# Filter copies between GpSimd's DMA issues in batch 0 of a fused Fourier filter and GELU MLP

## The chip, the cores and the metric

The kernel runs on one core of a Trainium2 chip. The metric is the device time of one execution in microseconds (us). TensorE is called PE, VectorE DVE, ScalarE ACT, GpSimd POOL, SyncE SP, as in the profile.

## The reference

`x` has 8 batches of 3008 rows and 256 columns. Each column is filtered in the frequency domain along the rows, and the result goes through an MLP with an exact GELU:

```
X = rfft(x, axis=1)
Y = X * (filt_r + 1j * filt_i)
y = irfft(Y, n=3008, axis=1)             # then reshaped to (24064, 256)
h = y @ w_in                              # (256, 2048)
g = 0.5 * h * (1 + erf(h / sqrt(2)))
out = g @ w_out                           # (2048, 256)
```

Inputs and output are float32. The filters have 1505 frequencies and 256 columns each.

## The kernel before

The transform of 3008 = 47 x 64 rows is done as matrix products in four stages, with tables of sines that the kernel computes at its start. The product with the filters lies in the middle. The MLP is done in tiles of 512 rows: `mm1` (line 711) makes a tile of `h`, ACT applies GELU into `g_sb` (line 714), and `mm2` (lines 727 and 793) multiplies by `w_out_sb`.

All order is written out by hand: each engine runs its instructions in the order in which the program names them, and instructions of different engines wait for each other by semaphores. Batch 0 goes first and alone. From batch 1 on, the stages of the next batch are put into numbered slots between the `mm1` and `mm2` of the present one; sixteen slots make a tile, and `mm2` of tile 0 begins in slot 10. The first stage of batch 1 (line 498) stands in slots 4, 8, 11 and 13, and its folds on DVE (lines 158 and 159) in slots 0, 1, 5 and 8.

The change is in batch 0. Its steps, with the lines of the profile:

- `load_x` (line 95): POOL issues eight DMAs that load batch 0 of `x` and cast it to bf16.
- `warm_up(n)` (line 375): `n` spare matmuls of 128 x 512 on PE, whose results nobody reads.
- `table_2_sin` (328), `table_2_swap` (335 on PE, copied by ACT), `table_3` (352, eight transposes on PE into one PSUM bank), `table_3_copy` (381 on ACT, into the tile `T3`), `table_3_turn` (368, two DVE instructions that make `T3i` out of `T3` with the parts swapped and signs turned), `table_4` (343): the tables. The trace shortens the names of these tiles to `T`.
- `c1` (606): the first stage, sixteen calls `u`, of four matmuls each, which are copied to `y_sb` in turn by DVE (383) and ACT (381).
- `load_filters(k0, k)` (168): POOL issues four DMAs for frequency groups `k0` to `k0 + k`: the real plane twice (32 partitions straight, 32 mirrored), then the imaginary plane twice. They fill partitions 0 to 63 of the tile `F`.
- `load_w_in` (211): two DMAs of 512 KB, one for each half of `w_in_sb`.
- `dup_filters(engine, k0, k)` (186): copies partitions 0 to 63 of `F` to 64 to 127, two groups at a time.
- `move_filters` (179): SP's DMAs that copy filters into the order `Fu` of the later batches.
- `c1t(q, ...)` (621): transposes of `y_sb` on PE, sixteen for `c1t(0)` and `c1t(1)` together, copied to `b_sb` by DVE or ACT.
- `c2(p)` (636, then 640 or 645 on DVE): two matmuls and the product with groups `2p` and `2p + 1` of `F`, for `p` from 0 to 11. Product `p` needs the filter copy of its two groups.
- `c3`, `c3t`, `c4` (658, 673, 687): the way back. Then come `mm1` and the slots.
- `load_x_pairs` (104): after its copies, POOL issues twelve DMAs with batch 1 of `x`, and then `load_w_out` (216), two DMAs of 512 KB, the first with the rows that `mm2` reads first.

POOL does its DMA issues and its copies in program order, and its DMAs go through one queue (software_dynamic). An issue also waits until an earlier DMA on the same semaphore has landed; there are eight such semaphores, taken in turn.

Before the change POOL issues all twelve filter DMAs and both of `w_in`, clears a corner of `vt_sb`, and then copies groups 6 to 23. Groups 0 to 3 are copied by DVE, groups 4 and 5 by ACT, after the last `c1`. DVE runs `table_3_turn(0)` after `c1` call 11.

Of the kernel before, what the change touches and what calls it, by code (L numbers as in the profile page):

```python
# [27 lines left out]
def _dram(src, off, dims):  # L28
    return dataclasses.replace(src, offset=src.offset + off, ap=[list(d) for d in dims])


class _Mix:
# [125 lines left out]
        tt(out=s[0:n], in0=x[0:n, 0, k], in1=x[0:n, 1, k], op=ALU.add)  # L158
        tt(out=x[0:n, 1, k], in0=x[0:n, 0, k], in1=x[0:n, 1, k], op=ALU.subtract)

    def load_filters(self, k0, k):

        nc, D = self.nc, self.D
        for t, src in enumerate((self.filt_r, self.filt_i)):
            direct = _dram(src, k0 * D, [[NA * D, 32], [D, k], [1, D]])
            mirror = _dram(src, (NA - k0) * D, [[NA * D, 32], [-D, k], [1, D]])
            for q, a in enumerate((direct, mirror)):
                nc.gpsimd.dma_start(out=self.F[32 * q:32 * q + 32, t, k0:k0 + k, :], in_=a)
# [36 lines left out]
                                     in_=_dram(self.x, 0, [[n, 2], [1, HB * self.D]]))  # L205
        self.load_x_mirror(b + 1, c, h)

    def load_w_in(self):
        wi = self.w_in.rearrange("(dc p) j -> p dc j", p=128)
        for dc in range(2):  # L210
            self.nc.gpsimd.dma_start(out=self.w_in_sb[:, dc, :], in_=wi[:, dc, :])

    def load_w_out(self, j):

# [647 lines left out]
def kernel(  # L862
# [9 lines left out]
    m = _Mix(ctx, tc, x, filt_r, filt_i, moe_w_in, moe_w_out, out)  # L872
    nc, B, S = tc.nc, m.B, m.S
# [6 lines left out]
    act = "act"  # L880
# [24 lines left out]
    t3 = m.pg.tile([128, 2, K1, 2, NB], BF16, tag="g", name="T3")  # L905
    m.T3, m.T3i = t3[:, 0], t3[:, 1]
    m.vt = m.pg.tile([128, 2, 97, 32], BF16, tag="g", name="vt_sb")
    for k, n in ((0, 6), (6, 8), (14, 10)):
        m.load_filters(k, n)
    m.load_w_in()  # L910

    nc.gpsimd.memset(m.vt[:, :, 96, :], 0.0)


    m.table_2_sin(0)
    for u in range(16):
        m.c1(u // 2, u % 2, False if u in (1, 3, 5, 7, 8, 10, 12, 14) else act)
        if u == 3:
            m.warm_up(3)
            m.table_2_swap(0)  # L920
            m.table_2_angle(g, 1)
            m.T1q = g.tile([2 * NA, K1, 2, 2], BF16, name="T1q")
            nc.vector.tensor_copy(out=m.T1q, in_=m.T1.rearrange("p (h r k) -> p k r h", h=2, r=2))
        if u == 7:
            m.table_2_sin(1)
            m.table_3(0)
            m.table_3_copy(0, 0)
            m.warm_up(2)
        if u == 11:
            m.table_2_swap(1)  # L930
            m.table_4(m.T4c, m.T1q, m.wtc, "n", False)
            m.table_3_turn(0)
            m.warm_up(1)
    m.table_3(1)
    m.dup_filters(nc.vector, 0, 2)
    m.dup_filters(nc.scalar, 4, 2)
    m.warm_up(1)
    m.c1t(0, (False, act))
    m.dup_filters(nc.vector, 2, 2)
    m.dup_filters(nc.gpsimd, 6, 18)  # L940
    m.move_filters(0, 2)
    m.c1t(1, (act,))
    m.table_3_copy(1, 0)
# [139 lines left out]
    for s in range((NT + 1) * 16):  # L1083
        t, jc = s // 16, s % 16
# [3 lines left out]
        if t - 1 in seven:  # L1088
            n = lambda i: (14 * i if i < 3 else 42 + 70 * (i - 3) // 13) if t == late else 7 * i
            m.mm2_seven(t - 1, n(jc), n(jc + 1))  # L1090
        elif t < 2:
            n = lambda i: max(4 * i - 40, 0) if i < 16 else min(24 + 8 * (i - 16) // 3, 64)
# [36 lines left out]
```

## Time and profile before

| | |
|---|---|
| time, median of 3 runs | 729.67 us (729.65 to 729.81) |
| profiled execution | 730.79 us |
| its span, first to last instruction | 728.7 us |
| PE busy | 712.0 us, 98% of the span |
| DVE, ACT, POOL busy | 84%, 79%, 35% |
| mean granted PE clock | 0.998 |
| chain that ended last | PE 93%, ACT 3%, others 1% or less |

The profile is of one execution, which took 1.12 us longer than the median of the timed ones. A row of a timeline has the start, the duration, the engine, the line, the operation, its tiles and shapes, and in square brackets how long the engine had been idle before it and what it then waited for. Ends of matmuls are modelled and overlap, so starts tell more than durations. Durations of POOL are rough.

### The profile page before, as it was taken

To read this page: it belongs to the slowest core of one execution; us is meant where nothing else is said; L and a number is where in the kernel's file an instruction comes from. 1 tells how busy PE (TensorE), PEld (TensorE's weight loads), DVE (VectorE), ACT (ScalarE), POOL (GpSimd) and SP (SyncE) were. 2 spreads that over 40 slices of the span, in tenths; PEclk is the share of its full clock that TensorE was granted. 3 is DMA by queue.
4 is the path that set the end of the run, shared out by engine and by line. 5 is a ranking of instruction groups with operands and counts; after the bars stand their busy time and mean duration, and the time that the engine had idled before them with its cause. 6 is when DMAs were issued, how large, how long until landed. Compare 5 with 4: busy or idle time off the path is not lost.

```text
span 728.7 us, 22436 instructions
## 1 busy us (share of the span) xinstructions
PE 712.0 (98%) x9189; PEld 507.4 (70%) x9341; DVE 613.4 (84%) x1105; ACT 576.6 (79%) x1050; POOL 256.9 (35%) x495
## 2 busy tenths in 40 slices
PE   8999999999999999999999999999999999999998
PEld 5856676666777666666777667666777767777776
DVE  7987788899998989898997999979988897765666
ACT  6998678788887888778887788877888788777773
POOL 7845847443232332223412242125521221121110
PEclk9999999999999999999999999999999999999999
DMA  9886634955257543665537654356545443311011
GB/s 154 157 179 145 160 95 118 238 135 116 82 166 193 124 110 97 187 151 134 127 104 190 144 132 122 88 153 158 104 101 140 139 123 100 94 47 43 31 58 59
DMA packets 88297, 91.05 MB, mean 125 GB/s; under 512 B 13169, under 2 KB 71537, under 8 KB 88193
## 3 DMA queue, kind: packets, MB, share of 16 engines
q1 hardware_dynamic: 63267, 51.21, 25.9%
q0 software_dynamic: 24512, 38.21, 23.4%
q8 instruction: 73, 1.20, 0.7%
q14 instruction: 29, 0.24, 0.1%
q10 hardware_dynamic: 416, 0.20, 0.1%
HBM read 57.48 MB, written 49.81 MB: 147 GB/s over the span
## 4 chain that ended last, share of the span: by engine, by line
PE 93%; ACT 3%; issue 1%; DVE 1%; DMA 1%; POOL 1%; DVEq 0%; POOLq 0%
PE ps_o L793 41%; PE ps_h L711 39%; PE ps_s L585 3%; PE ps_o L727 2%; ACT g_sb L714 2%; PE ps_s L556 2%; PE ps_s L525 2%; ACT y_sb L381 1%; DMA x_sb<-in_x_dram 1%; PE ps_s L498 1%; PE ps_s L142 1%; PE ps_c L658 1%; PE ps_warm L375 0%; PE ps_c L636 0%; PE ps_c1t L621 0%
## 5 line engine op out<-in xcount | busy, mean ns | idle before, releaser
L714 ACT ACTIVATE g_sb<-ps_h 128x512 f16<-128x512 f32 x752 | 446.1, 602 | 135.8 <-PE ps_h L711 111.4
L711 PE MATMUL ps_h<-y_sb,w_in_sb 128*128 128x512 bf16 (+3 forms) x1452 | 414.4, 365 | 0.7 <-ACT g_sb L714 0.3
L840 POOL DMA_DIRECT2D out_dram<-ost x219 | 124.2, 574 | 366.3 <-DVE ost L822 362.3
L793 PEld LDWEIGHTS <-g_sb 128*128 128x128 f16 x2880 | 188.8, 98 | 80.5 <-issue 12.4
L711 PEld LDWEIGHTS <-w_in_sb 128*128 128x128 bf16 x1600 | 125.6, 98 | 7.4 <-issue 1.6
L793 PE MATMUL ps_o<-w_sums,g_sb 128*128 128x128 f16 x1440 | 124.5, 219 | 1.6 <-DVE g_sb L765 0.2
L793 PE MATMUL ps_o<-w_sums,s_sb 128*128 128x128 f16 x1440 | 124.0, 219 | 1.8
L793 PEld LDWEIGHTS <-s_sb 128*128 128x128 f16 x1440 | 97.2, 98 | 38.0 <-issue 2.1
L759 DVE TENSOR_TENSOR s_sb<-g_sb 128x1024 f16<-128x1024 f16 x180 | 117.4, 683 | 1.0 <-ACT g_sb L714 0.6
L793 PE MATMUL ps_o<-w_out_sb,g_sb 128*128 128x128 f16 x1440 | 116.3, 219 | 1.9
L536 DVE TENSOR_TENSOR p<-ps_s,Fu 128x1024 bf16<-128x1024 f32 x84 | 101.7, 1217 | 13.7 <-PE ps_s L525 11.2
L765 DVE TENSOR_TENSOR g_sb<-s_sb,g_sb 128x1024 f16<-128x1024 f16 x90 | 61.7, 687 | 1.5
L793 PE MATMUL ps_o<-w_out_sb,F 128*128 128x128 f16 x704 | 60.6, 219 | 1.0
L775 DVE TENSOR_TENSOR F<-g_sb 128x1024 f16<-128x1024 f16 x88 | 60.0, 682 | 0.0
L793 PEld LDWEIGHTS <-F 128*128 128x128 f16 x704 | 47.1, 98 | 14.6 <-issue 0.4
L585 PEld LDWEIGHTS <-d_sb 96*128 96x128 bf16 x448 | 31.4, 97 | 26.7 <-issue 1.3
L822 DVE TENSOR_TENSOR ost<-t_sb,ps_o 128x256 f32<-128x256 f32 x88 | 32.9, 415 | 18.2 <-PE ps_o L793 18.2
L815 DVE TENSOR_TENSOR t_sb<-t_sb,ps_o 128x256 f32<-128x256 f32 x45 | 18.7, 416 | 32.2 <-PE ps_o L793 31.5
L381 ACT ACTIVATE y_sb<-ps_s 128x376 bf16<-128x376 f32 x95 | 45.4, 478 | 0.1
L381 ACT ACTIVATE F<-ps_s 128x512 bf16<-128x512 f32 x81 | 44.5, 608 | 0.1
L585 PE MATMUL ps_s<-F,d_sb 96*128 96x94 bf16 x448 | 37.2, 204 | 0.9
L810 DVE TENSOR_TENSOR ost<-t_sb,ps_o 128x256 f32<-128x256 f32 x45 | 18.6, 414 | 22.8 <-PE ps_o L793 22.8
(176 smaller groups left out, 630.3 us busy)
## 6 DMA issues: line engine op xcount, KB each, us to landing
out_dram<-ost POOLq DMA_DIRECT2D x117, 128.0 KB, 3.1
b_sb<-R SPq DMA_DIRECT2D x21, 512.0 KB
R<-F SPq DMA_DIRECT2D x84, 128.0 KB
R<-a_sb SPq DMA_DIRECT2D x108, 96.0 KB
d_sb<-R SPq DMA_DIRECT2D x54, 192.0 KB
x_sb<-in_x_dram POOLq DMA_DIRECT2D x36, 96.0 KB, 3.5
x_sb<-xr SPq DMA_DIRECT2D x32, 96.0 KB
x_sb<-in_x_dram POOLq DMA_DIRECT2D x12, 188.0 KB, 4.8
```

The costliest lines, as they stand in the source:

```text
L381: self.nc.scalar.activation(out=out, in_=in_, func=AF.Copy, scale=1.0 if scale is None else scale)
L536: v(out=w[:, a], in0=ps.unsqueeze(2).to_broadcast([128, 2, 2, 256]), in1=f.unsqueeze(1).to_broadcast([128, 2, 2, 256]), op=ALU.mult)
L585: nc.tensor.matmul(ps[:, 94 * i:94 * i + 94], lhsT=d[:, (grp % 2) * 4 + i, 128 * half:128 * half + 128], rhs=self.T4a[:, 4 * grp + i, 0:2 ...
L711: nc.tensor.matmul(ps[:, o:o + n], lhsT=w[:, dc], rhs=self.ring[:, dc, off:off + n], start=(dc == 0), stop=(dc == 1))
L714: nc.scalar.activation(out=self.st["g", t][:, jc, :], in_=ps, func=AF.Gelu)
L759: self.nc.vector.tensor_tensor(out=self.st["s", t][:, i:i + 2], in0=a, in1=b, op=ALU.subtract)
L765: self.nc.vector.tensor_tensor(out=a21[:, k], in0=self.st["s", t][:, k, 0], in1=a22[:, k], op=ALU.add)
L775: self.nc.vector.tensor_tensor(out=self.st["s4"][:, k], in0=a12[:, k], in1=s2[:, k], op=ALU.subtract)
L793: nc.tensor.matmul(ps[:, (m + 1) % 2, sub, :], lhsT=a[:, i, 128 * sub:128 * sub + 128], rhs=b[:, i], start=i == 0, stop=i == 7)
L815: v(out=t3, in0=t1, in1=p0, op=ALU.subtract)
L822: v(out=c(h, 1 - h), in0=tt, in1=p, op=ALU.add)
L840: eng.dma_start(out=out, in_=tile_[lo - r0:lo - r0 + n])
```

## The change

POOL issues the imaginary plane of the last filter groups only after it has copied groups 2 to 5, and `w_in` in two parts: the first half behind the copies of groups 6 to 15, the second behind those of groups 16 to 23. The clearing of `vt_sb` goes ahead of the filters. DVE keeps only the copy of groups 0 and 1, and makes it behind `c1t(0)`; ACT makes none. `table_3_turn(0)` goes behind the last `c1`. Two spare matmuls are added after the first swap and two before the wait for the second half of `x`, and one is removed ahead of `c1t(0)`.

```diff
-    def load_filters(self, k0, k):
+    def load_filters(self, k0, k, planes=(0, 1)):
...
-        for t, src in enumerate((self.filt_r, self.filt_i)):
+        for t in planes:
+            src = self.filt_i if t else self.filt_r
...
-    def load_w_in(self):
+    def load_w_in(self, dc):
         wi = self.w_in.rearrange("(dc p) j -> p dc j", p=128)
-        for dc in range(2):
-            self.nc.gpsimd.dma_start(out=self.w_in_sb[:, dc, :], in_=wi[:, dc, :])
+        self.nc.gpsimd.dma_start(out=self.w_in_sb[:, dc, :], in_=wi[:, dc, :])
...
-    for k, n in ((0, 6), (6, 8), (14, 10)):
-        m.load_filters(k, n)
-    m.load_w_in()
-
     nc.gpsimd.memset(m.vt[:, :, 96, :], 0.0)
-
+    m.load_filters(0, 6)
+    m.load_filters(6, 8)
+    m.load_filters(14, 10, (0,))
+    m.dup_filters(nc.gpsimd, 2, 4)
+    m.load_filters(14, 10, (1,))
+    m.dup_filters(nc.gpsimd, 6, 10)
+    m.load_w_in(0)
+    m.dup_filters(nc.gpsimd, 16, 8)
+    m.load_w_in(1)
...
             m.table_2_swap(0)
+            m.warm_up(2)
             m.table_2_angle(g, 1)
...
             m.table_3_copy(0, 0)
-            m.warm_up(2)
+            m.warm_up(4)
         if u == 11:
             m.table_2_swap(1)
             m.table_4(m.T4c, m.T1q, m.wtc, "n", False)
-            m.table_3_turn(0)
             m.warm_up(1)
+    m.table_3_turn(0)
     m.table_3(1)
+    m.c1t(0, (False, act))
     m.dup_filters(nc.vector, 0, 2)
-    m.dup_filters(nc.scalar, 4, 2)
-    m.warm_up(1)
-    m.c1t(0, (False, act))
-    m.dup_filters(nc.vector, 2, 2)
-    m.dup_filters(nc.gpsimd, 6, 18)
     m.move_filters(0, 2)
```

## The prediction, made before the change was run

> **What bounds the kernel now.** I read the page first: PE is busy 98% of the span and the chain that ended last is 93% PE. So a stage has room only where PE stands still or runs slowly, and whatever moves PE at the end of batch 0 moves the end by as much. Then I read the clock by stretches, the chain from 11 us, DVE and ACT up to the first product, POOL's queue, and the landing of `w_out`.
>
> The windows, in two stretches (busy time of each engine, granted clock, DMA share, GB/s):
>
> ```profile
> core 0: us, PE busy (x) PEld busy (x) DVE busy (x) ACT busy (x) POOL busy (x), PEclk, DMA share, GB/s
> 9.98:13.39 3.41, 2.15 (x26) 1.36 (x26) 1.77 (x5) 3.20 (x6) 1.45 (x4) 1.00 1.13 195
> 13.39:16.81 3.42, 3.42 (x33) 3.14 (x33) 2.36 (x7) 2.23 (x5) 3.42 (x7) 0.50 1.18 191
> ```
>
> After a stretch in which PE had 2.15 us of work, it runs 3.42 us at half clock. The chain there:
>
> ```profile
> 11.00 0.14 issue
> ...
> 13.35 1.11 PE ps_c L606 x12
> 14.46 0.85 PE ps_t L352 x8
> 15.32 0.43 PE ps_warm L375
> 15.74 1.46 PE ps_c1t L621 x16
> 17.20 0.23 PE ps_c L636 x2
> ```
>
> PE itself is the chain up to the first product. DVE and ACT wait there (idle before, in brackets):
>
> ```profile
> 13.21 0.34 DVE L368 TENSOR_SCALAR T<-T,turn_r 128x512 bf16<-128x512 bf16 x1
> 13.47 0.36 DVE L368 TENSOR_SCALAR T<-T,turn_i 128x512 bf16<-128x512 bf16 x1
> 13.76 1.00 DVE L383 CAST y_sb<-ps_c 128x384 bf16<-128x384 f32 x2
> 16.21 0.42 DVE L383 COPY b_sb<-ps_c1t 128x512 bf16<-128x512 bf16 x1 [0.83 <-PE ps_c1t L621]
> 17.46 1.23 DVE L640 TENSOR_TENSOR p<-ps_c,F 128x1024 bf16<-128x1024 f32 x1 [0.38 <-PE ps_c L636]
> ```
>
> From 17.46 DVE runs twelve products back to back, 1.13 us apart. POOL's queue decides what is loaded when:
>
> ```profile
> 14.81 1.26 POOL L168 DMA_DIRECT2D F<-in_filt_i_dram  x2
> 16.07 1.14 POOL L211 DMA_DIRECT2D w_in_sb<-in_moe_w_in_dram  x2
> 18.11 3.98 POOL L186 COPY F<-F 64x1024 bf16<-64x1024 bf16 x4 [0.74 <-DMA F<-in_filt_i_dram]
> 22.39 4.97 POOL L186 COPY F<-F 64x1024 bf16<-64x1024 bf16 x5 [0.31 <-DMA F<-in_filt_i_dram]
> 28.50 4.02 POOL L104 DMA_DIRECT2D x_sb<-in_x_dram  x8
> 36.09 1.53 POOL L216 DMA_DIRECT2D w_out_sb<-in_moe_w_out_dram  x2 [0.21 <-issue]
> ```
>
> Last, the tile `w_out_sb` (issue to landing), PE's first use of it, and the DMA share while its queue drains:
>
> ```profile
> DMA to landing us min/median/max: 7.6/8.6/9.6
> ```
>
> ```profile
> 45.05 0.79 PE L727 MATMUL ps_o<-w_out_sb,g_sb 128*128 128x256 f16 x4
> ```
>
> ```profile
> 26.00:28.50 2.50, 2.45 (x28) 1.90 (x27) 2.50 (x3) 2.50 (x5) 2.32 (x9) 1.00 0.18 49
> 30.00:40.00 10.00, 9.53 (x156) 8.21 (x156) 8.43 (x14) 9.42 (x22) 6.06 (x12) 1.00 0.95 172
> ```
>
> The first half of `w_out` is issued at 36.09 and lands 7.6 us later, at 43.7; PE reads it at 45.05. That slack of 1.3 us is what the change spends.
>
> **The front of batch 0.** *Spare matmul before L621:* one, 15.11 to 15.54 by start to start, leaves PE's chain. At half clock sixteen transposes then start at 15.11 and need 16 x 0.107 = 1.71 us, where they took 1.50 because the full clock came back at 16.81; the first product moves from 17.46 to 17.24, a gain of 0.22. *DVE's second filter copy* (0.42, from 16.67): DVE then waits 0.38 for PE anyway, so nothing yet. *ACT's copy* (1.04 at 15.02): ACT then waits 0.57, so nothing yet. *The turned copies* (two, 0.55 us by starts) let the last evictions start earlier, but PE reaches L621 only at 15.54, 0.55 after ACT's last eviction ended (14.99): nothing yet; in their new place DVE has 0.83 us idle. *L621 ahead of DVE's first filter copy* (0.42): that copy now runs behind L621's eviction, 16.41 to 16.83 by the slow clock, and the product waits for L636 until 17.24 anyway. These four count only if PE is faster.
>
> *Four spare matmuls,* 0.215 us each, go in before 11 us. Two meet a 0.30 us gap at 8.14 and delay the next L606 by 0.13; with two more PE ends near 10.56 instead of 10.0, and it waits for x until 11.0 anyway: free. They fill part of the 2.15 us stretch. If that keeps the clock full, from 13.35 eleven L606 matmuls go from 0.080 to 0.0425 apart (0.41), eight transposes from 0.107 to 0.056 (0.41), and the evictions become the chain: ACT's last one ends near 14.64 (PE at 14.02, two of 0.49, the earlier one begun at 13.7), L621 starts at 14.70, DVE's copy of its first half is at 15.14 to 15.56, the filter copy ends at 15.98, L636 at 16.0, the product starts at 16.05: a gain of 1.4. So 0.22 or 1.4. The table copy on DVE may stretch when POOL copies beside it (L745 ran 0.68 to 0.99 us with POOL copying), at most 0.3.
>
> The Trainium skill (TensorE: Matmul & The Clock Gate, Part 1) has the clock fall to half after an idle window of about 3.4 us and calls gaps under about 3 us harmless; the longest gap here is 0.97, so this trace disagrees, and by that rule the spare matmuls would buy nothing. It also calls the window free-running, which would let the dip come and go between runs.
>
> **POOL's queue.** The memset moves ahead of the filters (0.17, covered by the waits for x among their issues). After the tenth filter issue (14.82) POOL now makes two copies, 0.98 apart, until 16.95; their data landed by 14.96, when DVE's copy was released. The last two filter issues (1.26) end at 18.2 instead of 16.08. The packet record has the queue reach them at 18.06, and the first packet of the batch-1 load left 1.26 us after its issue began (28.50 to 29.76), so they begin at 18.2 and land near 22.45 instead of 22.35. Four copies fill 18.2 to 22.2; the fifth runs 22.5 to 23.5; `w_in` half 0 takes 0.57; four copies end at 28.0; `w_in` half 1 is issued at 28.0 instead of 16.6. The products keep their cover: the copy for product 8 ends at 25.05 and the product starts at 26.51 less the gain, so it stalls only for a gain above 1.45.
>
> What is late next: half 1 sits ahead of batch 1's x and of `w_out` in the same queue. Before, those megabytes went out in 20.1 to 25.5, and the engines then stood at 0.18 until 28.5. Now half 1 has its first packet at 28.0 + 1.26 = 29.26, needs 2.5 us (half 0: 20.13 to 22.65), and batch 1's x starts at 31.8 instead of 29.76: 2.0 late. The filter moves on SP took some 0.8 us of the engines beside x before, about 0.6 in the later window: 1.8 late. From 30 to 40 us the engines are 0.95 full, so nothing makes it up. Bounds: no delay at all if x flowed at `w_out`'s rate (195 KB/us against its own 147, 2.5 us less); 3.9 if the last filters landed the full 2.1 us later. I take 1.8, because the 0.95 row is of these very transfers. Batch 1's later x issues still wait for earlier landings (0.65 and 0.33 idle before), with the queue ahead of them full. `w_in` is safe (half 1 lands near 33.5, used at 38.8); the first half of x lands near 38.3 and DVE's fold, at 39.32 less the gain, wants it there: at most 0.4 of DVE, ahead of ACT-bound work. SP's filter moves wait for the last filters, 0.1 late, with no reader before slot 26.
>
> **Sum.** `w_out` half 0 lands at 43.7 + 1.8 = 45.5. PE would be ready at 45.05 less 0.22 or 1.4, and waits either way until 45.5: 0.45 us later than before. Everything behind it on PE (mm1 of the next slots, batch 1's stages) follows; PE has no gap to catch up. Profiled, 730.79 + 0.45 = 731.24 us (span 728.7, 2.1 around it); against the median of 729.67, which is 1.12 lower than the profiled execution, 730.1. About 0.2% (1.46 us) is what a measurement of this kernel can tell from no change; this lies inside.
>
> **Rivals.**
> *Slower: the timed runs have no half-clock stretch.* The 1.12 us between median and profiled execution is close to what the dip costs: without it L621 would start at 14.81, ACT's copy end at 16.06, the first product start at 16.28, 1.18 earlier. Then PE wants `w_out` at 43.87, just after it lands today, and gains only 0.23 from the change, while the load still comes at 45.5: 1.65 slower, 731.3. It decides beyond the bound once the load is over 1.6 late. Against: profiling may itself cost the 1.12. Chance 0.20.
> *Faster: the loads are not late and the clock stays full.* x drains faster or `w_out`'s slack is larger than read; the whole 1.4 arrives, less up to 0.3 for copies beside POOL: 728.3. For it: 0.86 us more work in the low stretch. Against: the 0.95 row. Chance 0.14.
> *It does not do what it says:* the clock still falls, and the loads are under 1 us late: 0.22 gain, 729.45. Chance 0.19.
> *Forecast:* `w_out`'s landing governs, 729.6 to 730.7 for delays of 1.2 to 2.3: chance 0.47.
>
> The range, 728.5 to 731.4, takes in the forecast, the small case, most of the slower rival and the near part of the faster one. Faster by over 0.2% needs all of the 1.4 and more: 0.06. Slower by over 0.2%: two thirds of the slower rival and the tail of late filters: 0.16. Within: 0.78.
>
> **What would show it.** Right: POOL issues the halves of `w_in` near 23.5 and 28.0, batch 1's x at 29.6 instead of 28.50; L727 waits for DMA of `w_out`, first at about 45.5. For the clock: no 0.50 stretch after 13.39, first L640 near 16.1 (17.2 if it stays). Wrong: L727 starts before 44.5 without waiting; L640 rows waiting for POOL; or the last filters landing after 23.3.

## The result, and the profile after

The changed kernel takes 732.36 us (median of 5, 732.04 to 732.90) against 729.65 us (median of 5, 729.29 to 729.81): 1.0038 times as long, 95% interval 1.0027 to 1.0049. It is 2.7 us slower, 2.3 more than forecast and above the end of the range. The profiled execution took 732.61 us with a span of 730.8 us.

The unchanged kernel was profiled once more (729.47 us, span 727.4), and so was the changed one (732.62 us, span 730.8); both showed a granted clock of 1.000. The profile of before that the prediction argued from was the odd one, with its half-clock stretch behind 13.39. So "before, again" is what the timed runs have to be compared with:

| us | before (first trace) | before, again | after | after, again |
|---|---|---|---|---|
| first product (L640) | 17.46 | 16.03 | 16.32 | 15.98 |
| `w_in` issues | 16.07, 16.61 | 15.73, 16.28 | 23.15, 27.64 | 23.27, 27.75 |
| first issue of batch 1's x | 28.50 | 28.07 | 29.29 | 29.39 |
| `w_in` half 1 lands | 26.75 | 26.28 | 33.85 | 33.27 |
| x's first DMA lands | 31.91 | 31.58 | 35.55 | 35.93 |
| x's fifth DMA lands | 35.81 | 35.36 | 39.58 | 39.68 |
| `w_out` issue | 36.09 | 35.64 | 39.87 | 39.96 |
| `w_out` half 0 lands | 43.72 | 43.12 | 47.34 | 47.35 |
| PE's first L727 | 45.05 | 43.70 | 47.38 | 47.39 |
| span | 728.67 | 727.37 | 730.82 | 730.85 |

"x" in the table and from here on is batch 1's, with its twelve DMAs. Landings are read from the semaphore events of the traces.

POOL's timeline of the kernel after (start, duration, engine, line, operation, tiles; in brackets the idle time ahead and its releaser). The changed file is one line longer, so L186 is now L187:

```profile
14.86 2.25 POOL L187 COPY F<-F 64x1024 bf16<-64x1024 bf16 x2 [0.20 <-DMA F<-in_filt_i_dram]
17.06 1.11 POOL L169 DMA_DIRECT2D F<-in_filt_i_dram  x2
18.23 4.97 POOL L187 COPY F<-F 64x1024 bf16<-64x1024 bf16 x5
23.15 0.56 POOL L211 DMA_DIRECT2D w_in_sb<-in_moe_w_in_dram  x1
23.70 3.98 POOL L187 COPY F<-F 64x1024 bf16<-64x1024 bf16 x4
27.64 0.54 POOL L211 DMA_DIRECT2D w_in_sb<-in_moe_w_in_dram  x1
29.29 3.52 POOL L104 DMA_DIRECT2D x_sb<-in_x_dram  x7
34.12 0.51 POOL L104 DMA_DIRECT2D x_sb<-in_x_dram  x1 [1.32 <-DMA w_in_sb<-in_moe_w_in_dram]
36.06 0.51 POOL L104 DMA_DIRECT2D x_sb<-in_x_dram  x1 [1.43 <-PE ps_c L687]
36.77 0.50 POOL L104 DMA_DIRECT2D x_sb<-in_x_dram  x1 [0.20 <-issue]
37.48 0.50 POOL L104 DMA_DIRECT2D x_sb<-in_x_dram  x1 [0.21 <-issue]
39.34 0.50 POOL L104 DMA_DIRECT2D x_sb<-in_x_dram  x1 [1.36 <-DMA x_sb<-in_x_dram]
39.87 1.53 POOL L216 DMA_DIRECT2D w_out_sb<-in_moe_w_out_dram  x2
```

The same stretch of before, again:

```profile
28.07 4.02 POOL L104 DMA_DIRECT2D x_sb<-in_x_dram  x8
32.45 0.50 POOL L104 DMA_DIRECT2D x_sb<-in_x_dram  x1 [0.36 <-PE ps_c3t L673]
33.30 0.50 POOL L104 DMA_DIRECT2D x_sb<-in_x_dram  x1 [0.34 <-DMA x_sb<-in_x_dram]
34.12 0.50 POOL L104 DMA_DIRECT2D x_sb<-in_x_dram  x1 [0.33 <-DMA x_sb<-in_x_dram]
34.83 0.50 POOL L104 DMA_DIRECT2D x_sb<-in_x_dram  x1 [0.20 <-issue]
35.64 1.53 POOL L216 DMA_DIRECT2D w_out_sb<-in_moe_w_out_dram  x2 [0.31 <-DMA x_sb<-in_x_dram]
```

Eight issues of x went in one piece before. Now the eighth stands still until the second half of `w_in` has landed, and the later ones wait longer than before. The profile puts the ninth's wait down to a PE matmul, and to another one in before, again; x's first DMA, on the same semaphore, had landed at 35.55, half a microsecond ahead of that issue.

The first x issue is 1.2 late; the `w_out` issue is 4.2 late. Besides following the last x issue in POOL's order, the `w_out` issue waits for a landing of its own. With eight semaphores taken in turn it has that of x's fifth DMA, and the profile's view of that one DMA (durations in ns, who waited for it, us to landing) names the waiter. First before, again, then after, again:

```profile
L104 POOL DMA_DIRECT2D x_sb<-in_x_dram x1: 506/506/506, 30.1 to 30.1; - x1
  POOL w_out_sb L216: 0.3, 1
DMA to landing us min/median/max: 5.3/5.3/5.3
```

```profile
L104 POOL DMA_DIRECT2D x_sb<-in_x_dram x1: 498/498/498, 31.4 to 31.4; - x1
  POOL w_out_sb L216: 0.2, 1
DMA to landing us min/median/max: 8.3/8.3/8.3
```

The fifth DMA of x is issued 1.3 later and takes 3.0 longer to land, and `w_out` is issued 0.28 behind that landing in both. No other wait of POOL stands ahead of the fifth DMA's issue. From there on nothing is lost: the issue-to-landing line of the tile `w_out_sb`, first of after, then of before, again.

```profile
DMA to landing us min/median/max: 7.5/9.0/10.5
```

```profile
DMA to landing us min/median/max: 7.5/8.4/9.3
```

The first half (the least of the three numbers) takes 7.5 us in both. PE's timeline of after, again, where the batch-0 work ends:

```profile
41.08 0.40 PE L498 MATMUL ps_s<-xs,T1s 47*64 47x512 bf16 x2 [1.76 <-DVE xs L158]
...
44.96 1.04 PE L711 MATMUL ps_h<-y_sb,w_in_sb 128*128 128x512 bf16 x4
47.39 0.60 PE L727 MATMUL ps_o<-w_out_sb,g_sb 128*128 128x256 f16 x4 [1.39 <-DMA w_out_sb<-in_moe_w_out_dram]
```

The same two places in before, again:

```profile
39.33 0.40 PE L498 MATMUL ps_s<-xs,T1s 47*64 47x512 bf16 x2
43.70 0.79 PE L727 MATMUL ps_o<-w_out_sb,g_sb 128*128 128x256 f16 x4
```

PE had waited for neither; now it waits 1.76 us for DVE's fold of batch 1's x and 1.39 us for `w_out`. The fold itself waits for x, as DVE's row of after shows:

```profile
40.37 0.69 DVE L158 TENSOR_TENSOR xs<-x_sb 111x1024 bf16<-111x1024 bf16 x1 [2.11 <-DMA x_sb<-in_x_dram]
```

The whole sequence stands in the chain of waits of after, again, read between 30 and 50 us:

```profile
30.91 8.03 DMA x_sb<-in_x_dram
38.94 0.28 issue
39.22 0.50 POOL x_sb L104
39.72 0.24 issue
39.96 7.38 DMA w_out_sb<-in_moe_w_out_dram
47.35 0.04 issue
47.39 0.60 PE ps_o L727 x4
```

A transfer of x, the fourth, releases POOL's last x issue. POOL then issues `w_out` (the 0.24 of "issue" ahead of it is the wait for the fifth, in POOL's timeline `[0.24 <-DMA x_sb<-in_x_dram]`), and its landing starts PE. L727 is 3.69 later and the span 3.48 longer.

### The profile page after: what moved, and what is told of

The parts are those of the page before. It is cut to its first block, busy times and chain, and to the rows that moved or that the text cites. A ratio compares the mean times of both kernels' runs of the same rounds, so it can differ in the third digit from the quotient of the medians.

```text
span 730.8 us, 22594 instructions
## 1 busy us (share of the span) xinstructions
PE 721.1 (99%) x9344; PEld 506.8 (69%) x9344; DVE 613.4 (84%) x1104; ACT 575.6 (79%) x1049; POOL 258.6 (35%) x497
## 4 chain that ended last, share of the span: by engine, by line
PE 96%; DVE 2%; DMA 1%; issue 0%; ACT 0%; POOL 0%; DVEq 0%
PE ps_h L711 44%; PE ps_o L793 39%; PE ps_s L585 3%; PE ps_o L727 2%; PE ps_s L525 2%; PE ps_s L556 2%; PE ps_s L498 1%; PE ps_s L142 1%; PE ps_c L658 1%; DMA x_sb<-in_x_dram 1%; PE ps_warm L375 1%; PE ps_c3t L673 0%; PE ps_c L636 0%; PE ps_c1t L621 0%; DVE y_sb L383 0%
## 5 line engine op out<-in xcount | busy, mean ns | idle before, releaser
L711 PE MATMUL ps_h<-y_sb,w_in_sb 128*128 128x512 bf16 (+3 forms) x1600 | 447.0, 367 | 0.0
L383 DVE CAST a_sb<-ps_s 128x512 bf16<-128x512 f32 x54 | 34.6, 681 | 3.4 <-PE ps_s L498 3.4
```

What stands on the lines that cost most here:

```text
L383: self.nc.vector.tensor_copy(out=out, in_=in_)
L711: nc.tensor.matmul(ps[:, o:o + n], lhsT=w[:, dc], rhs=self.ring[:, dc, off:off + n], start=(dc == 0), stop=(dc == 1))
```

## The experiments

The theory after the result: the slower kernel is the late place of `w_in` in POOL's queue; the rest of the change is worth a few tenths. The rivals: the front of batch 0 (copies of two engines beside each other, spare matmuls) lost the time; or x is short of transfer rate whatever the issues do. Each edit is against the kernel named in its diff; medians are given with the ratio to the kernel before of the same session (729.63 to 729.74 us).

**The two kernels again.** No edit.

> The kernel before, unchanged, for a second trace. Theory (its half-clock stretch in front of the first product is in few executions): granted clock near 1.000, first product (L640) at 16.0 to 16.3 instead of 17.46, L727 at 43.6 to 43.9 instead of 45.05, span near 727.4. Rival (the stretch belongs to the kernel): clock 0.998, first product at 17.4, span 728.7.

> The kernel after, unchanged, for a second trace, to set beside the second trace of the kernel before. Theory (the loss is the landing of x and w_out, with or without a half-clock stretch): w_out half 0 lands at 45.5 to 47.5, L727 waits for it, DVE's filter copy (L187) takes 0.75 to 0.87 us. Rival (the half-clock stretch at 41.8 in the first trace of after made its loss): without it L727 below 45.0 and a span under 728.9.

Measured: 729.47 and 732.62 us; the table above has the rest. The half-clock stretch at 13.39 did not come back, and L727 of before starts at 43.70. After's first trace had a half-clock stretch elsewhere (41.83 to 45.24), the second had none, and L727 began at 47.38 and 47.39: in after a dip there hides in the wait for `w_out`.

**Everything but `w_in`'s move.**

```diff
 # against after
     m.load_filters(14, 10, (1,))
+    m.load_w_in(0)
+    m.load_w_in(1)
-    m.dup_filters(nc.gpsimd, 6, 10)
-    m.load_w_in(0)
-    m.dup_filters(nc.gpsimd, 16, 8)
-    m.load_w_in(1)
+    m.dup_filters(nc.gpsimd, 6, 18)
```

> The kernel after, with both halves of w_in issued right behind the last filter DMAs and all nine later filter copies behind them. Theory (the late w_in delays batch 1's x and w_out): batch 1's x is issued near 29.3 with w_in already landed, w_out half 0 lands near 44.5 instead of 47.34, L727 starts near 44.5; the copies end 1.1 later, so product 3 starts near 20.4 and the front keeps about 0.5 of its 1.14 us; 729.0 to 729.6 us. Rival (the copies that POOL makes between its issues delay the stage): stays at 732 or above.

Measured: 729.97 us (n 11), 1.0006 [0.9998, 1.0015]. `w_out` is issued at 36.68 and lands at 44.31. PE's row:

```profile
44.47 0.79 PE L727 MATMUL ps_o<-w_out_sb,g_sb 128*128 128x256 f16 x4
```

The forecast of 729.0 to 729.6 was missed by 0.4: the 0.5 us of the front did not arrive. Some 2.4 of the 2.7 us are gone with this one edit. What is left, 0.34, can't be told from zero. x is issued at 29.18, about as in after (29.29), and its fifth DMA lands at 36.40 instead of 39.58, so x is not short of transfer rate by itself. In the trace product 3 could have started at 19.65 (18.52 + 1.13), but POOL's copy for it runs from 19.16 to 20.23, and it starts at 20.27, 0.62 late. Here the products do meet POOL, since the `w_in` issues stand ahead of the copies:

```profile
20.27 4.62 DVE L640 TENSOR_TENSOR p<-ps_c,F 128x1024 bf16<-128x1024 f32 x4 [0.53 <-POOL F L187]
```

**`w_in`'s move alone.**

```diff
 # against before
-    m.load_w_in()
...
-    m.dup_filters(nc.gpsimd, 6, 18)
+    m.dup_filters(nc.gpsimd, 6, 10)
+    m.load_w_in(0)
+    m.dup_filters(nc.gpsimd, 16, 8)
+    m.load_w_in(1)
```

> The kernel before, with nothing but w_in moved: half 0 behind POOL's fifth filter copy, half 1 behind its ninth. Theory: no front gain, w_out half 0 lands near 47.5 and L727 waits for it; 731.9 to 732.6 us, the whole loss of the change. Rival (the loss is in the copies or in the turned tables): 729.4 to 729.9.

Measured: 731.81 us (n 7), 1.0036 [1.0024, 1.0047]: 2.2 us slower by itself. The waits between 36 and 52 us (who waited for what: us in total, times, longest) have the same two as after, again, and shorter. L727 of this file is named L726:

```profile
DVE xs L158 <- DMA x_sb<-in_x_dram: 1.3, 1, 1.3
...
PE ps_o L726 <- DMA w_out_sb<-in_moe_w_out_dram: 0.8, 1, 0.8
```

The two experiments mirror each other: with the move 2.2 of the 2.7 us are there, a little less than the "whole loss" expected, and without it nearly none.

**The spare matmuls.** Once taken out of after, once put into before alone.

```diff
 # against after: none of the four
-            m.warm_up(2)      # behind table_2_swap(0)
-            m.warm_up(4)
+            m.warm_up(2)
 # against before: the four alone
+            m.warm_up(2)      # behind table_2_swap(0)
-            m.warm_up(2)
+            m.warm_up(4)
```

> The kernel after without the four added spare matmuls. Theory: the end of batch 0 is set by the landing of x and w_out, so PE's front does not matter: 732.0 to 732.7 us, L727 near 47.3 as before. Rival (the spares delay the first stage, 0.95 us of PE idle behind them): faster by 0.3 or more.

> The kernel before with only the four spare matmuls added. Theory (the clock is full there in nearly all executions anyway): 729.4 to 730.0 us, first product at 16.0 to 16.3. Rival (they prevent half-clock stretches that cost): 729.3 or less; or (they delay the first stage): 730.2 or more.

Measured: 732.72 us (n 5), 1.0036 [1.0023, 1.0049], without them, and 729.69 us (n 10), 1.0000 [0.9990, 1.0009], with them alone. They cost nothing that can be told, as predicted, and buy nothing. The profiled execution of the first (731.46) is the second fastest of its five, so its L727 at 45.91 need not stand for the others.

**`w_in`'s second half 4 us earlier,** right behind the first.

```diff
 # against after
     m.load_w_in(0)
+    m.load_w_in(1)
     m.dup_filters(nc.gpsimd, 16, 8)
-    m.load_w_in(1)
```

> The kernel after with half 1 of w_in right behind half 0, near 23.7 instead of 27.64; batch 1's x is still issued at 29.3. Theory: half 1 lands near 31, x starts about 2 us earlier than in the kernel after, w_out half 0 lands near 45.3, and the loss falls to about half: 730.4 to 731.3 us. Rival (the number of issues and copies ahead of x counts, which is the same): 732.0 to 732.6.

Measured: 730.21 us (n 10), 1.0005 [0.9995, 1.0015], 0.2 better than the range expected. The two issues leave at 23.13 and 23.68. All eight x issues now go in one piece, though x itself starts no earlier (29.32), and `w_out` is issued at 37.60, 2.3 earlier than in after and 0.28 behind the landing of x's fifth DMA. PE still waits, in the profiled execution, which at 730.74 us was the second slowest of its ten:

```profile
45.48 0.60 PE L727 MATMUL ps_o<-w_out_sb,g_sb 128*128 128x256 f16 x4 [1.37 <-DMA w_out_sb<-in_moe_w_out_dram]
```

So about 2.2 of the 2.7 us hang on the second half standing directly ahead of x.

**Batch 1's x issued 1.1 us earlier.**

```diff
 # against after: moved from ahead of the load_x_pairs loop
 # to behind its first part (c == 0)
+        if c == 0:
+            m.table_u_rows(g)
+            m.table_1_tiles(g)
```

> The kernel after with batch 1's first six x DMAs ahead of POOL's U and T1s rows, so that x is issued 1.07 us earlier, near 28.2. Theory (half 1 of w_in stands ahead in the queue, and the eighth x issue waits for its landing): that issue stays near 34, w_out half 0 lands within 0.6 of where it did, 731.7 to 732.5 us. Rival (POOL comes too late to the x issues): 1.0 us faster than the kernel after, near 731.3.

Measured: 731.14 us (n 10), 1.0021 [1.0012, 1.0030]. My theory's 731.7 to 732.5 missed, and the rival, POOL reaching the x issues too late, had it (731.3). x is issued at 28.20 and `w_out` at 37.84, 2.0 earlier than in after, although the eighth x issue still waits, until 33.45. So the eighth issue's wait for `w_in` is not what holds `w_out` up. It follows the fifth DMA of x, which was issued 1.1 earlier and landed 2.0 earlier, at 37.55. Why it gained more than the 1.1 is open.

**`w_out`'s first half between the x loads.**

```diff
 # against after
     for c in (0, 2):
+        if c:
+            m.load_w_out(0)
         for h in range(2):
             m.load_x_pairs(1, c, h, 2)
-    m.load_w_out(0)
```

> The kernel after with w_out's first half issued ahead of batch 1's second six x DMAs. Theory (the whole queue is late, x as much as w_out): w_out half 0 lands some 3 us earlier, but x lands later, the third fold waits for it with evictions of the first stage queued behind it on DVE, and L727 or the next slot waits for those: no faster than the kernel after, 732 to 734 us. Rival (only w_out's landing binds): 730.5 or less.

Measured: 734.93 us (n 4), 1.0070 [1.0051, 1.0089], the slowest of all, with the load of `w_out` early, at 42.06. Its expected range ended at 734. The profiled execution, 736.68, is the slowest of the four. PE's timeline:

```profile
45.62 0.27 PE L727 MATMUL ps_o<-w_out_sb,g_sb 128*128 128x256 f16 x1
...
48.83 0.80 PE L727 MATMUL ps_o<-w_out_sb,g_sb 128*128 128x256 f16 x3 [2.94 <-DVE a_sb L383]
```

and the cause in its waits:

```profile
DVE x_sb L158 <- DMA x_sb<-in_x_dram: 2.6, 1, 2.6
```

DVE stands at a fold of batch 1's x, which is now the last to land, and its next evictions are queued behind that fold. Bringing `w_out` forward moves the wait to x and makes it longer. Part of the time of this execution is the clock: from 47.75 on PE ran 6.83 us at half of it. The one run with a granted clock of 1.000 took 733.08, still not below after.

**POOL's two copies behind its last filter issues.**

```diff
 # against after
-    m.dup_filters(nc.gpsimd, 2, 4)
     m.load_filters(14, 10, (1,))
+    m.dup_filters(nc.gpsimd, 2, 4)
```

> The kernel after with POOL's two early filter copies behind the last two filter issues, not ahead of them. Theory (DVE's copy is stretched by POOL's copies beside it): DVE's copy L187 back to 0.42 to 0.50 us where POOL is still issuing, first product 0.3 earlier against the second stage's start; half 1 of w_in and x come no earlier, so the time stays at 731.5 to 732.5 us. Rival (the delay of the last filter issues makes the loss): 730.5 or less.

Measured: 731.60 us (n 10), 1.0029 [1.0019, 1.0039], in the median 0.8 less than after, with intervals that overlap, and 1.9 above before: the late filter issues don't make the loss. It also shows what copies of the two engines cost each other. In after, DVE copies beside POOL, and here alone, POOL starting at 15.98; the rows of DVE in after and in this kernel:

```profile
15.46 0.76 DVE L187 COPY F<-F 64x1024 bf16<-64x1024 bf16 x1
```

```profile
15.31 0.42 DVE L187 COPY F<-F 64x1024 bf16<-64x1024 bf16 x1
```

POOL's row in this kernel:

```profile
15.98 2.01 POOL L187 COPY F<-F 64x1024 bf16<-64x1024 bf16 x2
```

Alone they take 0.42 and 2.01 us; together, in after, 0.76 and 2.25.

**Two versions that might beat both.** Both keep the fewer copies on DVE and ACT and bring `w_in` forward again, between the copies; x is issued early as in the experiment with x 1.1 us earlier. The second also has POOL's first two copies behind the filter issues.

```diff
 # against after, first version (x as above)
-    m.dup_filters(nc.gpsimd, 6, 10)
+    m.dup_filters(nc.gpsimd, 6, 4)
     m.load_w_in(0)
-    m.dup_filters(nc.gpsimd, 16, 8)
+    m.dup_filters(nc.gpsimd, 10, 4)
     m.load_w_in(1)
+    m.dup_filters(nc.gpsimd, 14, 10)
 # second version: 6, 2 / 8, 4 / 12, 12, and the edit before this one
```

> The kernel after with half 0 of w_in behind two of POOL's seven later copies and half 1 behind four, and batch 1's first six x DMAs ahead of the U and T1s rows. Theory: the queue is never empty for long, x is issued near 28.2, w_out half 0 lands at or before 43.9, and L727 starts near 43.9: the front's 1.1 us arrives, 728.4 to 728.9 us. Rival (the landing of w_out follows something else than the queue's order): 730 or more.

> The kernel of e9 with half 0 of w_in behind POOL's third copy, half 1 behind its fifth, and batch 1's first six x DMAs ahead of the U and T1s rows. Theory (nothing of the change's cost is left, and the front gains at most the 0.46 us of DVE's second copy): x issued near 27.8, w_out half 0 landing at 43.2 or before, L727 near 43.5; 729.0 to 729.7 us. Rival (POOL's copies then hold up the products): 730 or more.

Measured: 729.38 us (n 11), 0.9998 [0.9989, 1.0007], and 729.54 us (n 10), 0.9997 [0.9988, 1.0006]. `w_out` is issued at 35.88 and 35.11, its half lands at 44.11 and 42.87, and L727 starts at 44.23 and 43.77, against 43.70 in before, again. Both win back the whole 2.7 us and neither beats the kernel before. The first was expected at 728.4 to 728.9 and missed: the front gained nothing, with the first product at 16.30 and 15.90 against 16.03. In the second PE starts L727 0.9 behind the landing of `w_out`, so an earlier load would not help it.

## Why the prediction was wrong, point by point

*What held.* The mechanism: L727 waits for the landing of `w_out`, put off by `w_in`'s place. POOL's times, too: `w_in` at 23.15 and 27.64 (predicted 23.5 and 28.0), x at 29.29 (29.6), the last filters landed at 21.25, earlier than the 22.45. The landing of `w_in`'s second half was right (33.27 and 33.85, predicted 33.5). No L640 row of after waits for POOL. The spare matmuls are free. DVE's copy stretched by 0.34 beside POOL (at most 0.3 was allowed for). None of the signs of being wrong that the prediction named came up.

*The term that was mis-sized: "1.8 us late".* The first half of `w_out` lands 3.6 later than in the first trace (43.72 to 47.34) and 4.2 later than in the second. The sum followed the bytes through the queue: 2.0 for the half of `w_in` ahead of x, less 0.2. By the rows of the table the whole delay is there when x's first DMA lands: 3.6 to 4.0 late against the first trace, 4.0 to 4.4 against the second. It hardly changes from there to the fifth DMA (3.8 to 4.3), the `w_out` issue and `w_out`'s landing. So the term is the delay of x itself, about double what the sum had.

Where it arises can be split. x's first DMA is issued 0.8 to 1.3 later and takes 6.3 to 6.5 us to land instead of 3.4 to 3.5. The sum's 1.8 puts that landing at 33.7, next to the landing of `w_in`'s second half at 33.5. It came 1.7 us behind that half in after and 2.7 in after, again. In the packet record (packets of 4 KB counted in order of their start, 128 for each half of `w_in`, then x) the half of `w_in` holds the queue for about 3.4 us until x's first packet, where the sum took 2.5. Why x's first packets then need 1.0 to 1.4 longer to land is open.

POOL's waits for landings, which the prediction called harmless, are not what made `w_out` late. The first seven x issues go out in one piece ahead of any wait, and the fifth already lands as late as `w_out` is issued. In 12 of the 14 traces the `w_out` issue stands 0.28 or 0.29 us behind that landing, whatever stood between. The exceptions are the kernel with `w_out` between the x loads and the one with `w_in`'s move alone (0.51). The `w_out` half landed 6.7 to 8.2 us after its issue in all the kernels but the one that issued it between the x loads (9.4).

The upper bound of 3.9 was about reached, but not for its reason, last filters that land late.

*A second wait that was counted too small.* "At most 0.4 of DVE" for the first half of x: it landed at 40.05 to 40.08 instead of 38.3, and DVE waited 2.11 and 2.37 us for it. PE lost 1.76 there. `w_out` came still later, so this wait is inside the other.

*The state of the clock, in the slower rival.* The forecast set the `w_out` delay against a slack of 1.3, from a trace with the half-clock stretch. The timed runs are like the trace without it: the first product is at 16.03 (the rival worked out 16.28), PE wants `w_out` at 43.70 (43.87), and the slack is 0.6. The rival's "against", that profiling may itself cost the 1.12 us, fell: the second profiled execution took 729.47. So the front's gain of 0.22 or 1.4 was nil (16.03 before, 15.98 and 16.32 after). The rival was right in kind, and its price of 1.65 too small mainly because it used the same 1.8. With the 4.2 measured, less 0.6, it gives 3.6, where L727 came 3.69 later and the span grew by 3.48. The medians differ by 2.7, between the two pairs of profiled executions (1.82 with the first trace, 3.15 with the second): executions of the kernel before alone ran from 729.3 to 731.0, and those of after from 732.0 to 732.9.

## What to carry to other kernels

An issue can wait for a landing that its data has nothing to do with: `w_out` reads nothing of x, and yet its issue stood behind x's fifth DMA, because they share a semaphore. When a transfer is moved back in a queue, find for each urgent issue behind it the landing that it waits for, and carry that landing's delay. Adding up bytes gave half of the delay here. And before a profile is used for a slack, compare its own time with the timed runs: here a profiled execution 1.1 us above the median had a half-clock stretch that the second one lacked, and with it more than double the slack that the change was going to spend. (The time alone does not tell: runs of the kernel before up to 730.99 had a granted clock of 1.000.) A transfer whose first reader is far off (the second half of `w_in`, read ten us later) is still not free to move if something urgent is queued behind it.

## What the runs showed of the hardware

A DVE copy of 64x1024 bf16 takes 0.42 to 0.51 us where POOL doesn't copy beside it, or only at its end, and 0.75 to 0.87 us in all eight traces of kernels where POOL copies in the same tile at that time. POOL's copy that starts during it then takes 1.23 us, and POOL's later ones 1.03 to 1.07. Whether it is the tile or something else that the two engines share was not tested.

The half-clock stretches of batch 0 began at 13.39 (first trace of before), 41.83 (first trace of after) and 47.75 (`w_out` between the x loads). The first two are 3.41 us long, the third 6.83. In the second trace of before, of the same program, there was none. The 3.41 us ahead of the three held 2.15, 1.60 and 1.55 us of PE work. Why the first of them, with no gap over 0.97 us, was enough is not shown; in after, again, 1.98 us of work in the 3.41 us from 39.98 brought none. The Trainium skill (TensorE: Matmul & The Clock Gate, Part 1) has the window free-running, and by that a dip that comes in one execution and not in the next is to be expected; the two traces agree with that. Its rule of no PE-idle gaps over about 3.4 us (the same part) would have had no dip in the first trace, and there was one.
